# A fused hash-attention and squared-ReLU kernel on one core: an earlier place for the second pair's hash work, and another spread of the sums of the input weights

## The chip, the cores and the metric

The kernel runs on one core of a Trainium2 chip. The metric is the time of one execution on the device in microseconds (us); "the time" of a kernel is the median over several executions. A profile is one more execution, recorded by the hardware profiler; times inside it are counted from the start of its span. TensorE is the matrix engine (PE in the profile), VectorE is DVE, ScalarE is ACT, GpSimd is POOL, and SyncE (SP) issues most of the DMAs.

## What is computed

Attention in which a query sees only the keys that have the same hash bucket, and then a feed-forward block with a squared ReLU. Cut to what matters:

```python
q, k, v: (4, 8, 768, 64); proj: (64, 6); w_in: (512, 2048); w_out: (2048, 512)

q_bits = (q @ proj > 0);  k_bits = (k @ proj > 0)
mask   = bucket(q_bits)[:, None] == bucket(k_bits)[None, :]
scores = where(mask, (q @ k.T) / 8, -1e9)
attn   = softmax(scores)
x      = (attn @ v), reshaped to (3072, 512)
out    = square(maximum(x @ w_in, 0)) @ w_out
```

## The kernel before

**Stages.** The attention comes first: 32 heads (4 batches of 8), two at a time, so 16 pairs (`pr` 0 to 15), about 330 us of the 880. The feed-forward block follows, as fast matrix multiplications of Strassen's kind: blocks of the inputs are added and subtracted first, and seven products stand for eight. The sums of blocks of `w_in` that these products need are made during the attention: 16 of them, `sum_in(0)` to `sum_in(15)`, each one VectorE operation on 128x512 numbers (lines 516 and 533) and two DMAs that write it to memory (`put_factor`, line 203). A dictionary `sums`, built by the loop that the change touches, says in which pair each is made: from pair 4 on (`NIN // 2`), when the first half of the input weights is there; what is left is made in the last pair.

**Order.** All engines' work is written in program order by hand (`tc.manual_schedule()`), with one queue per engine; the loop over the pairs below is that order.

**One pair.** The keys are cut into six tiles of 128 (`kt` 0 to 5).
- `features(pr, w)` (line 333): VectorE transposes the queries (w=0) and keys (w=1) of a pair in 32x32 blocks, so that features lie along the partitions; `nat` holds what the DMAs loaded (`load_pair`, issued two pairs ahead; the loads of pair 1 are issued at the start).
- `hash_bits(pr, banks)` (line 346): eight TensorE products of features with `proj` into one PSUM buffer, tile name `hash`.
- `signs(pr, w)` (line 356): eight ScalarE operations that read that buffer and write `bits`, keys first. `weigh(pr)` (line 382) scales the keys' bits.
- `prepare()`: `hash_bits` and both `signs` of the next pair.
- `score(pr, kt)` (lines 396 and 413): TensorE products of bits and of features into PSUM, 512 queries and then 256, each followed by ScalarE's exponential into `e`, one of a ring of four. PSUM buffers for scores and hash products come from one set of three, called `turn`, used in rotation.
- `add_up(pr, kt)` (lines 423 and 428): VectorE adds the exponentials of the tiles into `total`.
- `attend(pr, kt)` (line 438): TensorE products of exponentials and values, into one PSUM buffer `xo`.
- `finish(pr - 1)`: in the next pair, `sum_up` adds `total` over the partitions (line 455, `tot`; VectorE's `flip`, `once` and `both`, lines 460 to 466), the last two tiles are attended, and `spread` (line 477) distributes the reciprocals; `normalize` (lines 487 and 493, `recs` and `x_t`) scales and stores the result. The next pair's first `attend` needs `xo` free again.
- Beside this, pieces of the weights, given as 64-bit floats, are turned into 32-bit ones: `part_weight` (VectorE, lines 143 and 147), `place_power` (ScalarE, `small` and `power`, lines 160 and 161) and `round_weight` (VectorE, lines 171 to 179), for two pieces in a pair, `a` and `b`.

In pair 0 the loop differs: the pair's own hash bits are made ahead of the loop and within it (`first_keys`), the features of pair 1 are transposed after `add_up(0, 1)`, and `prepare()` for pair 1 runs after `score(0, 3)`. In the later pairs `features(pr + 1)` stands at the top of the pair and `prepare` runs inside `finish`, after `score(pr, 1)`.

After the last pair come `sum_x(0, 1)`, `finish(15)`, `normalize(15)`, and then the feed-forward block (`product`, line 712, and others).

Of the kernel before, what the change touches and what calls it, by code (L numbers as in the profile page):

```python
# [34 lines left out]
def kernel(  # L35
# [22 lines left out]
    NP = B * H // 2  # L58
# [45 lines left out]
    def turn(name):  # L104

        return ps_s.tile([P, 2, 512], FP32, name=name, tag="turn")
# [4 lines left out]
    NIN = 2 * NFT  # L111
# [11 lines left out]
    def load_weight(i):  # L123
        src, r, c = pieces[i]
        if src.dtype != U64:
            goals[i] = goal(i)
            nc.sync.dma_start(out=goals[i], in_=src[r:r + P, c:c + PIECE])
            return
        raw = p_w.tile([P, PIECE, 2], U32, name="raw", bufs=3)
        nc.sync.dma_start(  # L130
            out=raw.rearrange("p f w -> p (f w)"),
            in_=src.bitcast(U32)[r:r + P, 2 * c:2 * (c + PIECE)],
        )
        raws[i] = raw
# [28 lines left out]
    def round_weight(i):  # L163

        raw = raws.pop(i, None)
        if raw is None:
            return keep_weight(i)
        goals[i] = goal(i)
        low, high = raw[:, :, 0], raw[:, :, 1]
        power, top = parts.pop(i)  # L170
        nc.vector.scalar_tensor_tensor(  # L171
            out=power, in0=high, scalar=0x80000000, in1=power,
            op0=ALU.bitwise_and, op1=ALU.bitwise_or,
        )
        one = top.bitcast(FP32)
        nc.vector.scalar_tensor_tensor(
            out=one, in0=low, scalar=2.0**-32, in1=top, op0=ALU.mult, op1=ALU.add,
        )
        nc.vector.scalar_tensor_tensor(  # L179
            out=goals[i], in0=one, scalar=2.0**-20, in1=power.bitcast(FP32),  # L180
            op0=ALU.mult, op1=ALU.mult,
        )
        keep_weight(i)
# [95 lines left out]
    def load_pair(pr):  # L279


        b, j = divmod(pr, PB)
        for src, name in ((q, "q_nat"), (k, "k_nat")):
            t = p_qk.tile([P, S], FP32, name=name)
            for g in range(4):
                h, e = divmod(g, 2)
                nc.sync.dma_start(
                    out=t[g * 32:(g + 1) * 32].rearrange("i (c d) -> i c d", d=32),
                    in_=src[b, 2 * j + h].rearrange("(c i) (e d) -> e i c d", i=32, e=2)[e],
                )  # L290
            nat[pr, name] = t
# [38 lines left out]
    def features(pr, w):  # L330

        feat[pr, w] = p_f.tile([P, S], FP32, name=f"feat{w}")
        nc.vector.transpose(out=feat[pr, w], in_=nat[pr, ("q_nat", "k_nat")[w]])
# [3 lines left out]
    def hash_bits(pr, banks, ws=(0, 1), cs=(0, 1)):  # L337


        for w in ws:  # L340
            hashed[pr, w] = banks
            for c in cs:
                g = 2 * w + c
                for h in range(2):
                    rows = slice(h * D, (h + 1) * D)
                    nc.tensor.matmul(  # L346
                        out=banks[g * NR_B:(g + 1) * NR_B, h, 0:HS], lhsT=projs[rows],
                        rhs=feat[pr, w][rows, c * HS:(c + 1) * HS], start=True, stop=True,
                    )

    def signs(pr, w):
        bits[pr, w] = t = all_bits[pr % 2][w]
        for c in range(2):
            at = slice((2 * w + c) * NR_B, (2 * w + c + 1) * NR_B)
            for h in range(2):
                nc.scalar.activation(  # L356
                    out=t[h * D:h * D + NR_B, c * HS:(c + 1) * HS], in_=hashed[pr, w][at, h, 0:HS],
                    func=ACTF.Sign, scale=HUGE, bias=lifts[at],
                )
# [19 lines left out]
    def weigh(pr):  # L379

        t = bits[pr, 1]
        nc.scalar.activation(out=t, in_=t, func=ACTF.Copy, scale=gains)
# [3 lines left out]
    def score(pr, kt):  # L386

        e = ring[len(weights) % NRING]
        weights[pr, kt] = e
        key = slice(kt * P, (kt + 1) * P)  # L390
        sts = []

        def products(st, lo, hi, src, first):
            for h in range(2):
                rows = slice(h * D, (h + 1) * D)
                nc.tensor.matmul(  # L396
                    out=st[:, h, 0:hi - lo], lhsT=src[pr, 1][rows, key],
                    rhs=src[pr, 0][rows, lo:hi], start=first, stop=not first,
                )


        if (pr, kt) == (0, 0):
            for lo, hi in CUTS:
                sts.append(turn("st"))
                products(sts[-1], lo, hi, feat, True)
        for i, (lo, hi) in enumerate(CUTS):
            if len(sts) <= i:
                sts.append(turn("st"))
                products(sts[i], lo, hi, bits, True)
                products(sts[i], lo, hi, feat, False)  # L410
            else:
                products(sts[i], lo, hi, bits, False)
            nc.scalar.activation(  # L413
                out=e[:, :, lo:hi], in_=sts[i][:, :, 0:hi - lo], func=ACTF.Exp, scale=scale
            )
# [106 lines left out]
    def sum_in(m):  # L522

        c, n = divmod(m, 4)
        j, h = divmod(c, 2)
        t, at = ins[j], slice(h * NS, (h + 1) * NS)
        nf = NFT // 2
        a11, a12, a21, a22 = (
            t[:, f:f + nf, g, at] for g in range(2) for f in (0, nf)
        )  # L530
        s = in_sums[m] = p_t.tile([P, nf, NS], FP32, name=f"s_in{n}", bufs=2)
        if n == 0:
            nc.vector.tensor_tensor(out=s, in0=a21, in1=a22, op=ALU.add)
        else:
            minus(s, *(
                (in_sums[4 * c], a11), (a11, a21), (a12, in_sums.get(4 * c + 1))
            )[n - 1])
        put_factor((3, 4, 5, 6)[n], c * NS, s)
# [4 lines left out]
    todo = list(range(16))  # L543
    sums = {}
    for pr in range(NIN // 2, NP):
        n = 16 if pr == NP - 1 else 1 + (pr == NIN + 1)
        sums[pr], todo = todo[:n], todo[n:]

    xs = {}
# [1 line left out]
    def load_x(i):  # L551

        x = p_c.tile([P, NFT, NCH], FP32, name="x")
        nc.gpsimd.dma_start(out=x, in_=x_all[:, :, i * NCH:(i + 1) * NCH])
        xs[i] = x, [p_c.tile([P, 2, NCH // 2], FP32, name=f"t_x{n}") for n in range(3)]
# [36 lines left out]
    with tc.manual_schedule():  # L592
# [21 lines left out]
        for pr in range(NP):  # L614
            a, b = 2 * pr, 2 * pr + 1
            more = pr + 1 < NP

            def prepare():

                hash_bits(pr + 1, turn("hash"))  # L620
                for w in (1, 0):
                    signs(pr + 1, w)


            if pr + 2 < NP:
                load_pair(pr + 2)
            if pr == X_0:
                load_x(0)
            if more and pr > 0:
                for w in range(2):  # L630
                    features(pr + 1, w)
            if pr > 0:
                round_weight(b - 2)
                load_weight(b)
                for m in sums.get(pr, ()):
                    sum_in(m)
            score(pr, 0)
            if pr == 0:
                first_keys(1, turn("hash"))
            score(pr, 1)  # L640
            if pr > 0:
                finish(pr - 1, prepare if more else None)
            add_up(pr, 1)
            if pr == 0:
                for w in range(2):
                    features(1, w)
            if pr > 0:
                normalize(pr - 1)


            if pr == X_0 + 1:
                for n in range(2):
                    load_unit(n)
            part_weight(a)
            score(pr, 2)
            score(pr, 3)
            if pr == 0:
                prepare()
            elif more:
                weigh(pr + 1)  # L660
            place_power(a)
            attend(pr, 0)
            attend(pr, 1)
            for kt in (2, 3):
                add_up(pr, kt)
            if more:
                load_values(pr + 1)


            round_weight(a)  # L670
            part_weight(b)
            if more:
                load_weight(a + 2)
            score(pr, 4)
            score(pr, 5)
            if pr == 0:
                weigh(1)
            place_power(b)
            attend(pr, 2)
            attend(pr, 3)  # L680
            add_up(pr, 4)
            add_up(pr, 5)
# [801 lines left out]
```

## Time and profile before

| | us |
|---|---|
| time, median of five executions | 882.1 |
| the five executions | 880.24, 881.27, 882.1, 882.57, 883.03 |
| the profiled execution, whole | 881.76 |
| its span | 880.0 |
| pair 0 and what comes before it (0 to 30.03) | 30.03, TensorE busy 25.99, VectorE 17.62, ScalarE 20.92 |
| a middle pair with one sum (169.30 to 189.20) | 19.90, TensorE 19.90, VectorE 19.16, ScalarE 17.07 |
| the pair with two sums (189.20 to 209.10) | 19.90, TensorE 19.90, VectorE 19.13, ScalarE 17.07 |
| the last pair (308.60 to 332.70) | 24.10, TensorE 23.06, VectorE 23.61, ScalarE 11.56 |

How to read it: a row gives a stretch of the span and how long each engine was busy in it. An engine that is busy for the whole stretch sets its length; where none is, something waits for something else, and the timeline says for what. Lines of the timeline give the start, the duration, the engine, the line of the program, the operation, what it writes and reads, how many instructions of this kind stand together, and in brackets how long the engine was idle before it and what ended the idle time. Lines of a list of waits give who waited for whom, the sum in us, how often, and the longest. Matmul ends are modelled, and neighbours overlap.

### The profile page before, as it was taken

The numbers are of one execution on the slowest core, as the hardware profiler recorded it, in microseconds if no ns is written. First come the engines' busy times: TensorE is split into PE (matmuls) and PEld (weight loads), VectorE is DVE, ScalarE is ACT, GpSimd is POOL, SyncE is SP. The second block draws the span as 40 slices with busy tenths as digits, with TensorE's granted clock in tenths as the row PEclk, the third lists the DMA queues.
The fourth block names the chain that finished last, engine by engine and source line by source line (L and its number), as shares of the span: only waits on it lengthen the run. The fifth ranks groups of instructions, "written<-read, shape, count | busy, mean of one in ns | idle before, by whom it ended". The sixth has DMA issues, their size and how long they took to land.

```text
span 880.0 us, 12132 instructions
## 1 busy us (share of the span) xinstructions
PE 865.2 (98%) x4340; PEld 519.4 (59%) x4340; DVE 760.8 (86%) x1099; ACT 391.6 (45%) x673; POOL 106.9 (12%) x172
## 2 busy tenths in 40 slices
PE   8999999999999999999999999999999999999996
PEld 3444444444444444444688865556888755568885
DVE  5899999999999998888779968888889788888875
ACT  5988888888888851222211123332111233321110
POOL 2000000000000000554231011111000211210002
PEclk9999999999999999999999999999999999999999
DMA  9678976898778536989897665436857744355565
GB/s 184 128 150 135 231 151 150 180 260 219 180 168 221 164 124 205 302 260 289 290 350 246 177 158 173 166 117 226 287 146 189 169 162 156 125 167 154 157 176 103
DMA packets 224131, 167.09 MB, mean 190 GB/s; under 512 B 164448, under 2 KB 181344, under 8 KB 224064
## 3 DMA queue, kind: packets, MB, share of 16 engines
q1 hardware_dynamic: 189152, 87.19, 40.9%
q0 software_dynamic: 12528, 41.30, 15.2%
q10 hardware_dynamic: 22384, 37.76, 13.8%
q8 instruction: 36, 0.59, 0.3%
q14 instruction: 31, 0.25, 0.1%
HBM read 124.52 MB, written 41.68 MB: 189 GB/s over the span
## 4 chain that ended last, share of the span: by engine, by line
PE 94%; DVE 2%; ACT 1%; issue 1%; DMA 1%; ACTq 0%; DVEq 0%
PE acc L712 40%; PE st L396 17%; PE acc L931 16%; PE xo L438 13%; PE acc L884 5%; PE hash L346 1%; PE tot L455 1%; DVE total L428 1%; DMA k_nat<-in_k_dram 1%; ACT e L413 1%; ACT bits L356 1%; DVE s_in L516 0%; DVE out_piece L179 0%; DVE power L171 0%; ACT small L160 0%
## 5 line engine op out<-in xcount | busy, mean ns | idle before, releaser
L413 ACT ACTIVATE e<-st 128x1024 f32<-128x1024 f32 x192 | 145.1, 810 | 45.0 <-PE st L396 41.0
L396 PE MATMUL st<-feat,feat 64*128 64x512 f32 (+1 forms) x768 | 150.4, 483 | 0.0
L438 PE MATMUL xo<-e,v_nat 128*64 128x512 f32 (+1 forms) x768 | 134.8, 492 | 0.0
L712 PE MATMUL acc<-b,leaf 128*128 128x256 f32 x600 | 133.2, 379 | 1.3 <-issue 1.3
L712 PEld LDWEIGHTS acc<-b,leaf 128*128 128x128 f32 x600 | 113.8, 190 | 17.7 <-issue 2.3
L428 DVE TENSOR_TENSOR total<-total,e 128x1536 f32<-128x1536 f32 x64 | 112.4, 1756 | 5.2 <-ACT small L160 0.5
L438 PEld LDWEIGHTS xo<-e,v_nat 128*64 128x64 f32 x768 | 51.3, 136 | 82.4 <-issue 74.6
L931 PE MATMUL acc<-t_x,w_unit 128*128 128x512 f32 x192 | 90.2, 592 | 0.0
L396 PEld LDWEIGHTS st<-feat,feat 64*128 64x128 f32 x768 | 66.0, 188 | 33.3 <-issue 23.4
L712 PE MATMUL acc<-t,leaf 128*128 128x256 f32 x336 | 76.2, 380 | 0.0
L356 ACT ACTIVATE bits<-hash,lifts 32x384 bf16<-32x384 f32 x120 | 68.6, 572 | 3.2 <-issue 1.3
L712 PEld LDWEIGHTS acc<-t,leaf 128*128 128x128 f32 x336 | 63.7, 190 | 9.1 <-DVE t L516 0.5
L796 DVE SCALAR_TENSOR_TENSOR b<-h 128x512 f32<-128x512 f32 x96 | 65.7, 691 | 3.0
L396 PE MATMUL st<-bits,bits 64*128 64x256 bf16 (+1 forms) x384 | 63.2, 325 | 1.8 <-ACT e L413 1.4
L931 PE MATMUL acc<-x,w_unit 128*128 128x512 f32 x128 | 60.1, 592 | 0.0
L712 PE MATMUL acc<-x,w_unit 128*128 128x512 f32 x128 | 56.6, 594 | 0.0
L712 PE MATMUL acc<-b_t,leaf 128*128 128x256 f32 x240 | 53.8, 379 | 0.0
L931 PEld LDWEIGHTS acc<-t_x,w_unit 128*128 128x128 f32 x192 | 36.5, 190 | 28.9 <-issue 26.8
L719 ACT COPY two<-acc 128x256 f32<-128x256 f32 (+1 forms) x29 | 12.5, 431 | 87.8 <-PE acc L712 75.3
L719 ACT COPY one<-acc 128x256 f32<-128x256 f32 (+1 forms) x29 | 12.5, 431 | 86.3 <-PE acc L712 48.3
L712 PEld LDWEIGHTS acc<-b_t,leaf 128*128 128x128 f32 x240 | 45.5, 190 | 6.2
L396 PEld LDWEIGHTS <-bits 64*128 64x128 bf16 x384 | 23.5, 93 | 42.0 <-issue 37.9
(159 smaller groups left out, 1166.9 us busy)
## 6 DMA issues: line engine op xcount, KB each, us to landing
leaf<-w_out ACTq DMA_DIRECT2D x142, 256.0 KB, 3.0
w_unit<-w_in SPq DMA_DIRECT2D x16, 640.0 KB, 3.9
raw<-in_moe_w_in_dram SPq DMA_DIRECT2D x16, 512.0 KB, 5.5
raw<-in_moe_w_out_dram SPq DMA_DIRECT2D x16, 512.0 KB, 4.4
w_unit<-w_in SPq DMA_DIRECT2D x8, 896.0 KB, 8.0
w_out<-sums POOLq DMA_DIRECT2D x16, 448.0 KB, 6.8
sum<-w_in SPq DMA_DIRECT2D x16, 448.0 KB, 4.8
v_nat<-in_v_dram SPq DMA_DIRECT2D x16, 384.0 KB, 4.8
```

The source lines that it names most:

```text
L346: nc.tensor.matmul(out=banks[g * NR_B:(g + 1) * NR_B, h, 0:HS], lhsT=projs[rows], rhs=feat[pr, w][rows, c * HS:(c + 1) * HS], start=True, ...
L356: nc.scalar.activation(out=t[h * D:h * D + NR_B, c * HS:(c + 1) * HS], in_=hashed[pr, w][at, h, 0:HS], func=ACTF.Sign, scale=HUGE, bias=li ...
L396: nc.tensor.matmul(out=st[:, h, 0:hi - lo], lhsT=src[pr, 1][rows, key], rhs=src[pr, 0][rows, lo:hi], start=first, stop=not first,)
L413: nc.scalar.activation(out=e[:, :, lo:hi], in_=sts[i][:, :, 0:hi - lo], func=ACTF.Exp, scale=scale)
L428: nc.vector.tensor_tensor(out=totals[pr], in0=totals[pr], in1=weights[pr, kt][:, :, 0:S], op=ALU.add)
L438: nc.tensor.matmul(out=xo[h * D:(h + 1) * D, lo:hi], lhsT=nat[pr, "v_nat"][:, h, kt * D:(kt + 1) * D], rhs=weights[pr, kt][:, h, lo:hi], s ...
L455: nc.tensor.matmul(out=tot[g * 32:(g + 1) * 32, 0:HS], lhsT=ones, rhs=totals[pr][:, h, c * HS:(c + 1) * HS], start=True, stop=True,)
L712: nc.tensor.matmul(out=acc[to], lhsT=a(i), rhs=b(i), start=first and i == 0, stop=last and i == n - 1, skip_group_check=True,)
L719: nc.scalar.copy(out=t, in_=acc[of])
L796: nc.vector.scalar_tensor_tensor(out=out, in0=h, scalar=0.0, in1=h, op0=ALU.max, op1=ALU.mult)
L884: nc.tensor.matmul(out=out, lhsT=w[:, a], rhs=b, start=start, stop=stop, skip_group_check=True)
L931: nc.tensor.matmul(out=acc[to], lhsT=w[:, PLACE[a], f], rhs=bt[b](f), start=first and f == 0, stop=last and f == NFT // 2 - 1, skip_group_ ...
```

## The change

Three edits in the order of the work. First, the loop that builds `sums`: before, the pair `NIN + 1` (index 9, the tenth) makes two sums and every other one from index 4 to 14 makes one, which leaves four for the last. After, the pairs with an index divisible by three (6, 9 and 12) make two, which leaves two for the last. Second, in pair 0 the two `features` of pair 1 move ahead of `add_up(0, 1)` on VectorE. Third, in pair 0 `prepare()` for pair 1 moves ahead of `score(0, 3)`: on TensorE the eight hash products come before the products of tile 3, on ScalarE the eight signs before its two exponentials. The instructions are the same in number and kind on every engine.

```diff
     for pr in range(NIN // 2, NP):
-        n = 16 if pr == NP - 1 else 1 + (pr == NIN + 1)
+        n = 16 if pr == NP - 1 else 1 + (pr % 3 == 0)
         sums[pr], todo = todo[:n], todo[n:]
...
             score(pr, 1)
+            if pr == 0:
+                for w in range(2):
+                    features(1, w)
             if pr > 0:
                 finish(pr - 1, prepare if more else None)
             add_up(pr, 1)
-            if pr == 0:
-                for w in range(2):
-                    features(1, w)
             if pr > 0:
                 normalize(pr - 1)
...
             part_weight(a)
             score(pr, 2)
-            score(pr, 3)
             if pr == 0:
                 prepare()
-            elif more:
+            score(pr, 3)
+            if more and pr > 0:
                 weigh(pr + 1)
             place_power(a)
             attend(pr, 0)
```

## The prediction

> **What bounds the kernel now.** I read the engine totals and the chain that ended last, then all that TensorE waited for in the whole run, then the timelines of single engines around those waits.
>
> ```profile
> PE 865.2 (98%) x4340; PEld 519.4 (59%) x4340; DVE 760.8 (86%) x1099; ACT 391.6 (45%) x673; POOL 106.9 (12%) x172
> ...
> PE 94%; DVE 2%; ACT 1%; issue 1%; DMA 1%; ACTq 0%; DVEq 0%
> ```
>
> TensorE is the kernel. A change of order pays only where TensorE stands still; here is the complete list:
>
> ```profile
> PE xo L326 <- DVE excess L235: 1.5, 1, 1.5
> PE st L396 <- ACT e L413: 1.4, 2, 1.2
> PE acc L712 <- issue: 1.3, 1, 1.3
> PE tot L455 <- DVE total L428: 1.0, 1, 1.0
> PE acc L1039 <- DVE o L1008: 0.8, 1, 0.8
> PE hash L346 <- ACT e L413: 0.6, 1, 0.6
> PE st L396 <- ACT bits L356: 0.4, 1, 0.4
> ```
>
> Lines 2, 6 and 7 (2.4 us) are in the first pair, line 4 (1.04 us) is the end of the last pair. Between them TensorE has no gap at all: the sums of a pair (L455) begin every 19.91 us, thirteen times on end (34.31 to 293.10). So the first half of the change can gain a part of 2.4 us, the second half a part of 1.04 us, and nothing else is to be had. First pair, ScalarE, then VectorE:
>
> ```profile
> 13.32 4.75 ACT L413 ACTIVATE e<-st 128x1024 f32<-128x1024 f32 x6 [0.85 <-PE st L396]
> 19.39 4.66 ACT L356 ACTIVATE bits<-hash,lifts 32x384 bf16<-32x384 f32 x8 [1.33 <-issue]
> 24.08 0.72 ACT L160 ACTIVATE small<-power,excess 128x512 uint8<-128x512 uint32 x1
> ```
>
> ```profile
> 13.01 0.38 DVE L374 TENSOR_SCALAR bits<-bits,spans,bases 128x384 bf16<-128x384 bf16 x1
> 14.86 1.76 DVE L423 SCALAR_TENSOR_TENSOR total<-e,e 128x1536 f32<-128x1536 f32 x1 [1.48 <-ACT e L413]
> ...
> 17.43 0.94 DVE L333 STREAM_TRANSPOSE feat<-k_nat 128x768 f32<-128x768 f32 x1
> ...
> 25.50 0.69 DVE L171 SCALAR_TENSOR_TENSOR power<-raw,power 128x512 uint32<-128x512 uint32 x1 [2.95 <-ACT power L161]
> ...
> 32.53 0.94 DVE L333 STREAM_TRANSPOSE feat<-k_nat 128x768 f32<-128x768 f32 x1
> ```
>
> The reader is to see: VectorE waits 1.48 us for an exponential and only then transposes the next pair's features; so the hash products come late, ScalarE idles 1.33 us before their signs, and everything queued behind the signs (small, power, the exponential of tile 4 at 25.49) is late; TensorE waits 1.21 us for that exponential. Last pair, VectorE and TensorE:
>
> ```profile
> 312.80 0.69 DVE L516 TENSOR_TENSOR s_in<-in 128x512 f32<-128x512 f32 x1
> 313.40 0.68 DVE L516 TENSOR_TENSOR s_in<-in,s_in 128x512 f32<-128x512 f32 x1
> 314.00 0.58 DVE L460 STREAM_TRANSPOSE flip<-tot 128x384 f32<-128x384 f32 x1
> ...
> 316.64 0.98 DVE L487 STREAM_TRANSPOSE recs<-xo 128x768 f32<-128x768 f32 x1
> ...
> 319.26 3.62 DVE L428 TENSOR_TENSOR total<-total,e 128x1536 f32<-128x1536 f32 x2
> ```
>
> ```profile
> 329.07 0.85 PE L455 MATMUL tot<-total,ones 128*32 128x384 f32 x8 [1.04 <-DVE total L428]
> ```
>
> From 309.54 to 329.02 VectorE runs with no pause above 0.1 us: here it sets the end.
>
> **What the Trainium skill says.** "PSUM — Partial Sum Buffer", section Engine vs sequencer instructions: ScalarE's and VectorE's queues are strict FIFO, and matmuls start and complete in program order. The trace agrees: small (24.08) and the tile-4 exponential stand behind the eight signs although tile 4's products were done at 23.7. "VectorE: DVE Perf Modes", section The TRN2 errata: an fp32 tensor_tensor takes (N+151)/0.96 ns; that is 691 for N=512 and 1757 for 1536, and the rows have 0.69 and 1.76. "ScalarE: Activation LUTs", section What ACT_TABLE_LOAD costs: neighbouring ACTIVATEs overlap by about 93 ns. The exponentials do (0.11: 13.32+1.03 against 14.24), the signs do not (eight of 0.572 take 4.66).
>
> **First pair, step by step.** Nothing is added or removed: two transposes, eight hash products and eight signs move. VectorE: the two transposes go ahead of L423. It is free at 13.39; the two take 1.83 (16.54 to 18.37), so they end at 15.25. Their inputs: the last k_nat DMA was issued at 8.3 and the tile's DMAs took 3.6 to 5.6, so it is there by 13.9 at worst. TensorE: the products of tile 2 are issued by 15.26, when the hash products now come; they take 0.81 (292.29 to 293.10 in pair 14). Their PSUM turn (three buffers) is the one that tile 1's second exponential left at 14.83. They are done at about 16.2, and tile 3's products follow at 16.1, when tile 2's first exponential has freed a turn (15.96). ScalarE: tile 2's exponentials end at 16.45, signs from 16.48 to 21.14 (4.66), tile 3's exponentials to 22.69, small from 22.57 (they overlap by 0.1), power from 23.33, tile 4's first exponential from 23.98 to 25.01. Before it ended at 26.52. TensorE meanwhile: tile 3 to 17.8, attention products of tiles 0 and 1 (2.74) to 20.5; then a new wait, as tile 4's turn is the hash turn: to 21.19, 0.6 us, hidden because the wait behind it is longer. The second half of tile 5 starts at 25.06 against 26.57: **1.51 us sooner**.
>
> But the exponentials of tile 3 are now behind the signs, and VectorE's add of tile 3 (second L428) waits for them: 22.72 to 24.48, in place of 20.79 to 22.55. L171 behind it starts at 24.39, not 25.50: VectorE gains only **1.11**. From there to the transposes of pair 2 it runs without a break (25.50 to 33.47), so these end at 32.36. TensorE reaches the hash products of pair 2 at 33.30-1.51 = 31.79; its key half started at 33.53 before (0.23 behind the query half, at 33.30) and will start at 32.42, 0.63 behind. So 0.40 of the gain is given back and TensorE follows VectorE: 1.11 us. Bounds: 1.51 if key features don't hold TensorE there, 0.7 if the signs start 0.4 later than I think (several semaphores in one wait). I take 1.11.
>
> **Pairs 7, 10, 13.** The tenth has two sums before and after. A sum costs VectorE 0.60 start to start (313.40 to 314.00), ahead of the flip. What hides it: VectorE has some 0.75 us to spare in a 19.91 us pair (19.15 busy), and the trace has the very case: in the tenth pair with two sums, both ended at 196.01 and its reader on TensorE (L477) began at 196.98; x_t ended at 199.63, the attention products that need its bank began at 200.51; the next L455 came after 19.91 as ever. Margins 0.97 and 0.88. So nothing for the seventh and thirteenth, at most 0.3 each if they lie worse. On SP two more small issues (0.90 for two at 134.74) stand ahead of the x_all write and the v_nat load; the values are read a pair later. POOL's order is the same.
>
> **Last pair.** Two of four sums go, 1.2 us of VectorE. The flip can't come before the sums' products: L455 at 312.20, and in pairs 2 to 8 the flip starts 0.91 to 0.92 after it, so at 313.12: 0.88 gained. recs needs L477, which TensorE does at 315.62, 0.30 before recs in pair 14 (296.51, 296.81): 315.92, 0.72 gained. x_t, L143, L147 follow to 318.54; the add of tile 2 needs the exponential that ends at 318.61 (ScalarE, paced by TensorE): 318.65 against 319.26, **0.61 gained**. Afterwards nothing bites: power is ready at 321.50 (needed 322.19), tile 4's exponential at 324.69 (needed 324.79), tile 5's at 326.31 (needed 326.65). The sums' products start at 328.46; TensorE is free at 328.03, so 0.43 of its wait stays. Bounds: 0.3 to 1.04, the whole wait.
>
> **Sum.** 1.11 + 0 + 0.61 = 1.72 off the span of 880.0: 878.28. The profiled execution took 881.76, 1.76 outside the span, so 880.04; it lay 0.34 below the median of 882.1, from which 1.72 leaves 880.4. That is 0.195%, all but at the 0.2% (1.76 us) that a measurement of this kernel can tell from no change. The later stages keep their order on every engine and shift as a whole.
>
> **Rivals.** *More:* the key half of pair 2's hash isn't on the path, because later matmuls absorb its 0.4 us. For it: TensorE lists no wait there before. Against: L455 of that pair came 0.78 after the key half, as tight as can be. 1.51+0.61 = 2.12: 880.0. With the whole last wait gone too, 879.5. *Only one half bites:* the last pair's adds are held by ScalarE alone, or the first pair's gain is eaten by VectorE's lag: 0.6 to 1.1, 881.0 to 881.5. For: both gains are what is left after a second wait. *Slower:* the hash products now stand ahead of tile 3 on TensorE and the signs ahead of tile 3's exponentials on ScalarE. If k_nat or VectorE is late, both queues stop, one for one once the key products end after 16.4. At 18.1 the total gain is gone; with the old feature times they end at 19.3 to 20.1, some 3.7 late: 2 us slower, 884.1. Against: the data are there 1.2 to 1.3 us early by the median landing (3.9).
>
> **How the numbers follow.** Forecast 0.58, more 0.25, one half 0.10, slower 0.07. A spread of half a microsecond around 880.4 puts the forecast's weight evenly on both sides of the bound: 0.28 faster, 0.30 same. More is faster (0.24; 0.01 same); one half is same (0.10). Faster 0.52, same 0.41, slower 0.07. The bounds of the unknown costs give gains of 1.0 to 2.55, so 879.5 to 881.1; the five runs before lay from 880.24 to 883.03, which moves a median by some 0.7 either way: 878.8 to 881.9.
>
> **What would show it.** Right: TensorE's waits in the first pair some 0.6 and 1.0 at tile 4 and the second half of tile 5, none at the hash; signs starting at about 16.5; pair 2's L455 at about 33.2; later L455s 19.91 apart; the last wait about 0.4. Wrong: signs after 17.5, a gap before tile 3, a wait at pair 7 or 13, or an L455 of pair 2 at 32.8 (then "more").

## The result, and the profile after

The changed kernel takes 879.68 us (median of 22 executions) against 881.49 us for the kernel before (43 executions). The ratio is 0.9979, with a 95% interval from 0.9974 to 0.9985: 1.8 us less, 0.21%. The forecast was 1.72 us less.

First the list of all that TensorE waited for in the changed kernel (who waited for whom, sum in us, times, longest):

```profile
PE xo L326 <- DVE excess L235: 1.5, 1, 1.5
PE st L396 <- ACT e L413: 1.2, 2, 1.0
PE acc L1039 <- DVE o L1008: 0.8, 1, 0.8
PE tp L309 <- DMA k_nat<-in_k_dram: 0.8, 1, 0.8
PE acc L712 <- issue: 0.6, 1, 0.6
PE st L396 <- ACT bits L356: 0.5, 1, 0.5
PE tot L455 <- DVE total L428: 0.4, 1, 0.4
```

The wait ahead of the hash products is gone. The one for the signs (0.4 before, 0.5 now) has moved from tile 5 to tile 4. Both start as soon as the signs are done with reading a PSUM buffer: at 24.11 before (signs until 24.05), at 21.24 now (signs until 21.19). At the end of the last pair 0.4 of 1.04 us is left. A new line, 0.8 us for the keys at the very start, and a smaller one in the feed-forward block (L712: 0.6 instead of 1.3) differ between executions of one kernel, as the last experiment and the last section show.

The timeline of ScalarE in the first pair:

```profile
13.37 3.13 ACT L413 ACTIVATE e<-st 128x1024 f32<-128x1024 f32 x4 [0.85 <-PE st L396]
16.52 4.67 ACT L356 ACTIVATE bits<-hash,lifts 32x384 bf16<-32x384 f32 x8
21.21 1.51 ACT L413 ACTIVATE e<-st 128x1024 f32<-128x1024 f32 x2
22.75 0.72 ACT L160 ACTIVATE small<-power,excess 128x512 uint8<-128x512 uint32 x1
```

ScalarE no longer idles ahead of the signs; they start at 16.52 instead of 19.39. But tile 3's two exponentials (21.21; before, they were done at 18.07) now stand behind them. VectorE shows who waits for those:

```profile
13.37 0.97 DVE L333 STREAM_TRANSPOSE feat<-q_nat 128x768 f32<-128x768 f32 x1
14.27 0.94 DVE L333 STREAM_TRANSPOSE feat<-k_nat 128x768 f32<-128x768 f32 x1
...
22.76 1.76 DVE L428 TENSOR_TENSOR total<-total,e 128x1536 f32<-128x1536 f32 x1 [3.58 <-ACT e L413]
24.43 0.69 DVE L171 SCALAR_TENSOR_TENSOR power<-raw,power 128x512 uint32<-128x512 uint32 x1
...
31.48 0.94 DVE L333 STREAM_TRANSPOSE feat<-k_nat 128x768 f32<-128x768 f32 x1
```

VectorE waits 3.58 us for tile 3, adds it, and L171 follows at once, without a wait of its own: the add holds it. The key transposes of pair 2 end at 32.42. TensorE before:

```profile
17.66 1.62 PE L346 MATMUL hash<-feat,projs 64*32 64x384 f32 x16 [0.60 <-ACT e L413]
...
24.11 0.39 PE L396 MATMUL st<-bits,bits 64*128 64x512 bf16 x2 [0.37 <-ACT bits L356]
...
26.57 0.29 PE L396 MATMUL st<-bits,bits 64*128 64x256 bf16 x2 [1.21 <-ACT e L413]
...
33.30 1.08 PE L346 MATMUL hash<-feat,projs 64*32 64x384 f32 x16
34.31 0.85 PE L455 MATMUL tot<-total,ones 128*32 128x384 f32 x8
```

And after:

```profile
15.42 0.88 PE L346 MATMUL hash<-feat,projs 64*32 64x384 f32 x16
...
21.24 0.39 PE L396 MATMUL st<-bits,bits 64*128 64x512 bf16 x2 [0.48 <-ACT bits L356]
...
25.10 0.29 PE L396 MATMUL st<-bits,bits 64*128 64x256 bf16 x2 [0.99 <-ACT e L413]
...
31.83 1.49 PE L346 MATMUL hash<-feat,projs 64*32 64x384 f32 x16
33.25 0.85 PE L455 MATMUL tot<-total,ones 128*32 128x384 f32 x8
```

Tile 5's second half starts 1.47 us sooner (25.10 against 26.57). The listed waits between `first_keys` and there have shrunk by only 0.73 us (from 2.42 to 1.69). The other 0.74 was inside the hash products of pair 1, which took 1.62 us before and take 0.88 now: their key half waited for VectorE's transposes (it started at 18.43, the transposes ended at 18.37), and the list of waits does not show a stop within such a group.

The hash products of pair 2, though, stretch over 1.49 us instead of 1.08, as their key half (from 32.47) waits for the transposes, and L455 is 1.06 sooner (33.25 against 34.31). From there every pair takes what it took: thirteen steps of 19.91. In the last pair, VectorE and then TensorE:

```profile
311.01 0.68 DVE L516 TENSOR_TENSOR s_in<-in,s_in 128x512 f32<-128x512 f32 x1
312.06 0.58 DVE L460 STREAM_TRANSPOSE flip<-tot 128x384 f32<-128x384 f32 x1 [0.37 <-PE tot L455]
...
314.85 0.98 DVE L487 STREAM_TRANSPOSE recs<-xo 128x768 f32<-128x768 f32 x1
...
317.59 3.62 DVE L428 TENSOR_TENSOR total<-total,e 128x1536 f32<-128x1536 f32 x2
```

```profile
327.40 0.85 PE L455 MATMUL tot<-total,ones 128*32 128x384 f32 x8 [0.43 <-DVE total L428]
```

The flip now waits for TensorE: VectorE has more time than it can use here. The last L455 comes at 327.40 (329.07 before), so 0.61 is added to the 1.06. The spans differ by more, 2.3 us (880.0 and 877.7): beside these 1.67 us, the L712 gap is 0.72 smaller.

### The profile page after: what moved, and what is told of

Same layout as the page of the kernel before. It is cut to its first block, busy times and chain, and to the rows that moved or that the text cites. A ratio compares the mean times of both kernels' runs of the same rounds, so it can differ in the third digit from the quotient of the medians.

```text
span 877.7 us, 12130 instructions
## 1 busy us (share of the span) xinstructions
PE 864.4 (98%) x4340; PEld 518.6 (59%) x4340; DVE 760.4 (87%) x1099; ACT 391.5 (45%) x673; POOL 107.0 (12%) x172
## 4 chain that ended last, share of the span: by engine, by line
PE 95%; DVE 2%; ACT 1%; DMA 1%; issue 0%; ACTq 0%; DVEq 0%
PE acc L712 40%; PE st L396 17%; PE acc L931 16%; PE xo L438 14%; PE acc L884 6%; PE hash L346 2%; PE tot L455 1%; DVE total L428 1%; DMA k_nat<-in_k_dram 1%; ACT bits L356 1%; ACT e L413 0%; PE xo L477 0%; DVE x_t L493 0%; PE tp L309 0%; DVE recs L487 0%
## 5 line engine op out<-in xcount | busy, mean ns | idle before, releaser
L712 PE MATMUL acc<-b,leaf 128*128 128x256 f32 x600 | 133.3, 379 | 0.6 <-issue 0.6
L712 PEld LDWEIGHTS acc<-b,leaf 128*128 128x128 f32 x600 | 113.8, 190 | 17.2 <-issue 1.9
L712 PE MATMUL acc<-t,leaf 128*128 128x256 f32 x336 | 76.2, 380 | 0.0
L712 PEld LDWEIGHTS acc<-t,leaf 128*128 128x128 f32 x336 | 63.7, 190 | 9.1 <-DVE t L516 0.5
L712 PE MATMUL acc<-x,w_unit 128*128 128x512 f32 x128 | 56.6, 594 | 0.0
L712 PE MATMUL acc<-b_t,leaf 128*128 128x256 f32 x240 | 53.8, 379 | 0.0
L712 PEld LDWEIGHTS acc<-b_t,leaf 128*128 128x128 f32 x240 | 45.5, 190 | 6.2
```

Of the source, the lines that this page charges most:

```text
L712: nc.tensor.matmul(out=acc[to], lhsT=a(i), rhs=b(i), start=first and i == 0, stop=last and i == n - 1, skip_group_check=True,)
```

## Experiments

Pair 0 gets going up to 0.6 us sooner in one execution than in another (the last section shows how), and all of it shifts with that. The table therefore counts from the start of the second hash product group of pair 0 (`first_keys`, at 10.96 before). All numbers are from the timelines, in us; the last two columns are the first step between two L455, and TensorE's wait ahead of the last L455.

| kernel | `first_keys` at | tile 5, second half | L171 | first L455 | first step | last wait |
|---|---|---|---|---|---|---|
| before | 10.96 | 15.61 | 14.54 | 23.35 | 19.91 | 1.04 |
| the change | 11.02 | 14.08 | 13.41 | 22.23 | 19.91 | 0.43 |
| sums only | 10.95 | 15.60 | 14.53 | 23.33 | 19.91 | 0.42 |
| first pair only | 11.46 | 14.09 | 13.42 | 22.22 | 19.91 | 1.03 |
| features only | 11.45 | 14.29 | 13.23 | 22.03 | 19.91 | 0.42 |
| next features sooner | 11.22 | 14.07 | 13.41 | 21.61 | 20.27 | 0.43 |

Six profiles are of kernels with the first pair as in the change: it itself, first pair only, and the last four below. Their first L455 lies at 22.20 to 22.25, so a difference of less than 0.05 says nothing.

### The two halves apart

Sums only: the kernel before with

```diff
-        n = 16 if pr == NP - 1 else 1 + (pr == NIN + 1)
+        n = 16 if pr == NP - 1 else 1 + (pr % 3 == 0)
```

> The kernel before with the other spread of the sums alone. Theory (two separate gains that add up): pair 0 as before, sums of pair 1 (L455) first at about 34.3 us, fourteen intervals unchanged, TensorE's wait ahead of the last L455 down from 1.04 to 0.43 us, so 0.6 us less in all, ratio about 0.9993. Rival (one half carries all): ratio 1.000, the wait at the last L455 still 1.0, because VectorE starts the last pair late when TensorE is not ahead.

Measured: ratio 0.9995 (0.9987 to 1.0004); the last wait falls from 1.04 to 0.42, everything before it stays. First pair only: the changed kernel with that line turned back.

> The changed kernel with the sums as in the kernel before. Theory: TensorE's waits in pair 0 are 0.5 and 1.0, none at the hash products; first L455 at about 33.25 (before: 34.31), all later ones 1.06 us sooner than before, last wait 1.04 as before; 1.06 us less, ratio about 0.9988. Rival (VectorE's lag from pair 0 grows when the last pair keeps four sums): last wait above 1.04 and less than 1 us gained.

Measured: ratio 0.9986 (0.9978 to 0.9995); first L455 1.13 sooner in the table, last wait 1.03. The halves add up, 0.62 and 1.13, and neither needs the other. The time alone could not have said so for the sums: its interval holds no change, and only the wait shows the gain.

### The third edit alone taken back

```diff
             score(pr, 2)
+            score(pr, 3)
             if pr == 0:
                 prepare()
-            score(pr, 3)
```

> The changed kernel with the hash products and signs of pair 1 back behind tile 3, so of the first-pair edits only the earlier transposes are left; sums as in the change. Theory (VectorE's add of tile 3 behind the signs gives back 0.4 us): signs start at about 18.1 us instead of 19.39, tile 5's second half at about 25.3, VectorE's L171 at about 24.2, and the first L455 at about 33.0, that is some 0.2 us sooner than in the full change (33.25): the third edit loses on balance. Rival (the third edit carries the gain, TensorE's time in pair 0 decides): tile 5's second half 0.2 us later than in the full change and the first L455 at 33.45 or later.

Measured: ratio 0.9978 (0.9971 to 0.9985). VectorE in the first pair of this kernel:

```profile
17.86 3.62 DVE L428 TENSOR_TENSOR total<-total,e 128x1536 f32<-128x1536 f32 x2
24.68 0.69 DVE L171 SCALAR_TENSOR_TENSOR power<-raw,power 128x512 uint32<-128x512 uint32 x1 [3.20 <-ACT power L161]
```

The two adds run together again, and L171 waits for ScalarE's power. In the table tile 5 is 0.21 later than with the full change, as the rival has it, and L171 0.18 and L455 0.20 sooner, as the theory has it. (Times from the span's start are some 0.45 above the expected ones, since pair 0 began 0.49 later. L455 at 33.48 would meet the rival's "33.45 or later" for this reason alone.) So the earlier transposes bring 1.32 us by themselves. The third edit helps TensorE by 0.21 in pair 0 and costs VectorE 0.18, and VectorE is what counts one pair later: by these profiles the change would be 0.2 us better without it. The times do not tell the two kernels apart (879.57 and 879.68); the statement rests on the profiles.

### The features of the pair after that, sooner too

```diff
-            if more and pr > 0:
+            if more and pr > 1:
                 for w in range(2):
                     features(pr + 1, w)
...
+            if pr == 0:
+                for w in range(2):
+                    features(2, w)
             add_up(pr, 4)
             add_up(pr, 5)
```

> The changed kernel with the transposes of pair 2's features moved from the top of pair 1 to before the adds of tiles 4 and 5 in pair 0. Theory (in pair 1 TensorE follows VectorE's transposes, which ate 0.4 us): hash products of pair 2 no longer split in two halves, first L455 at about 32.65 instead of 33.25, later ones the same 0.6 us sooner, ratio to the kernel before about 0.9972. Rival (the key half of the hash was not on the path, or the adds of tiles 4 and 5 now come too late for L455): first L455 stays at 33.2 or goes later, ratio 0.998 or above.

Measured: ratio 0.9978 (0.9971 to 0.9985). TensorE in pair 1 of this kernel:

```profile
32.02 0.88 PE L346 MATMUL hash<-feat,projs 64*32 64x384 f32 x16
32.83 0.85 PE L455 MATMUL tot<-total,ones 128*32 128x384 f32 x8
...
36.66 1.02 PE L396 MATMUL st<-feat,feat 64*128 64x512 f32 x4
37.87 0.29 PE L396 MATMUL st<-bits,bits 64*128 64x256 bf16 x2 [0.19 <-ACT bits L356]
```

The hash products take 0.88 in one piece, and L455 is another 0.62 sooner: the key half was on the path, as forecast. But the next step is 20.27, so 0.36 is given back. Tile 2's second half (37.87) now waits for the signs of pair 2, which end at 37.82; it starts 1.21 us after the products before it. In the changed kernel:

```profile
37.08 1.02 PE L396 MATMUL st<-feat,feat 64*128 64x512 f32 x4
37.94 0.27 PE L396 MATMUL st<-bits,bits 64*128 64x256 bf16 x2
```

There the same products start after 0.86 us, although the signs run until 38.07. In the trace that instruction waits for a semaphore that ScalarE raises here, and for one that TensorE raises in the change. So it has probably been given another of the three PSUM buffers, the one that the signs still read. Net gain over the change by the profile 0.26; in the time it does not show (879.73).

### How many sums the pairs can hide

None in the last pair, two in each pair of odd index from 5 to 13:

```diff
-        n = 16 if pr == NP - 1 else 1 + (pr % 3 == 0)
+        n = 16 if pr == NP - 1 else 1 + pr % 2
```

> The changed kernel with two sums in every pair of odd index from 5 to 13 (the sixth to the fourteenth pair), none in the last. Theory (in the last pair two sums are already hidden: the flip waits for TensorE's L455, then recs for L477, then the adds for the exponentials): flip of the last pair but one still 0.92 after its L455, last wait still 0.43, no gain over the change. Rival (each sum taken from the last pair is worth its 0.6 us): the last wait gone, another 0.4 us and more. In the pairs with two sums L455 steps of 19.91 as ever.

Measured: ratio 0.9982 (0.9975 to 0.9989), all steps 19.91, last wait 0.43. VectorE in the last pair:

```profile
310.10 0.69 DVE L179 SCALAR_TENSOR_TENSOR out_piece<-top,power 128x512 f32<-128x512 f32 x1
312.36 0.58 DVE L460 STREAM_TRANSPOSE flip<-tot 128x384 f32<-128x384 f32 x1 [1.57 <-PE tot L455]
```

The flip's wait grew from 0.37 to 1.57 by just the two sums (1.20), and nothing else moved: those two were hidden, as the forecast had it. Three in the last pair (two in the seventh and tenth alone):

```diff
-        n = 16 if pr == NP - 1 else 1 + (pr % 3 == 0)
+        n = 16 if pr == NP - 1 else 1 + (pr in (6, NIN + 1))
```

> The changed kernel with two sums in the seventh and tenth pair only, so three in the last. Theory (three sums end at 313.4 on the clock of the kernel before, 0.3 after the flip could start, and later waits swallow that): last wait 0.43 to 0.5, so nearly all of the gain with one sum moved instead of two. Rival (0.3 us for each sum): last wait 0.7.

Measured: ratio 0.9982 (0.9974 to 0.999), last wait 0.43. One sum moved out of the last pair had all of the gain; the second brought nothing. Four in the tenth pair, one in the others, two in the last:

```diff
-        n = 16 if pr == NP - 1 else 1 + (pr % 3 == 0)
+        n = 16 if pr == NP - 1 else 1 + 3 * (pr == NIN + 1)
```

> The changed kernel with four sums in the tenth pair and one in each other pair from the fifth to the fourteenth, two in the last. Theory (0.6 us a sum, margins of 0.97 and 0.88 with two): with two more sums VectorE comes 1.2 us later, past both margins, so the spread products (L477) and the first attention products of that pair wait, and the one L455 step behind the tenth pair is 20.2 to 20.3 instead of 19.91; all others 19.91. Rival (VectorE has hidden room for any number, as it waits for exponentials anyway): 19.91 there too.

Measured: ratio 0.9987 (0.9978 to 0.9996); the step behind the tenth pair is 20.28, all others 19.91. VectorE there, then TensorE:

```profile
194.41 0.68 DVE L533 TENSOR_TENSOR s_in<-in 128x512 f32<-128x512 f32 x1
195.01 0.57 DVE L460 STREAM_TRANSPOSE flip<-tot 128x384 f32<-128x384 f32 x1
...
198.66 1.02 DVE L493 SCALAR_TENSOR_TENSOR x_t<-xo,recs 128x768 f32<-128x768 f32 x1
```

```profile
196.12 0.30 PE L477 MATMUL xo<-both,picks 128*64 128x24 f32 x4
...
199.74 2.81 PE L438 MATMUL xo<-e,v_nat 128*64 128x512 f32 x16
```

Four sums are past the cover: L477 starts at 196.12 behind `both` (195.88 to 196.06), and the attention products at 199.74, after x_t's end at 199.68. Two sums beyond the two are 1.20 us of VectorE and cost 0.37, so 0.83 was covered, near the smaller of the two margins forecast (0.88), and the rival with room for any number falls. Three sums in such a pair were not run.

### The changed kernel once more

> The changed kernel unchanged, for a second profile of it. Theory (the gap ahead of a product of the feed-forward block near 450 us and the first arrival of the keys at 6.5 us differ from run to run and have nothing to do with the change): L455 steps and waits in the pairs as in the first profile within 0.02 us, that gap somewhere from 0.5 to 1.3, the second first_keys product from 10.9 to 11.5. Rival (the change moved the gap): again 0.58 within 0.05.

Measured, in one execution: steps and waits in the pairs as in the first profile (first L455 22.23 after `first_keys`; waits of 0.49, 0.99 and 0.42). TensorE's wait for the keys, 0.8 in the first profile, is not in the list. The L712 gap was 0.97, against 0.58 in the first profile.

```profile
PE acc L712 <- issue: 1.0, 1, 1.0
```

So 0.4 of the 2.3 us between the two spans lies within what that gap does between two executions of the same kernel. That the rest of its 0.72 is chance too is likely, not shown: the changed kernel had 0.58 and 0.97, the kernel before 1.30 in its one profile, but sums only 0.90, and four in the tenth 1.63. What TensorE waits for there the profile does not show ("issue").

## Why the prediction was right

- *The first pair's VectorE and ScalarE.* Predicted: key features done at 15.25, signs from 16.48, tile 4's exponential from 23.98. Measured 15.21, 16.52 and 24.04. The closeness of the last is part luck: small and power came 0.18 later than forecast (22.75 and 23.51), since small did not overlap the exponentials before it, and the exponential then began 0.10 before power's end, which was not forecast. The two waits left on TensorE were put at 0.6 and 1.0; they are 0.48 and 0.99, with the first one, new at tile 4, hidden behind the second as forecast.
- *The list called complete.* The prediction took 2.4 us as all that the first half could gain. That is wrong both ways: 0.24 of it lies at tile 1 (12.03 before, 0.22 left after), which no edit touches, and 0.74 within the hash products of pair 1 is not in the list. The forecast did not suffer, as it was worked out along ScalarE's queue.
- *The part of the gain that is given back.* Predicted: TensorE gains 1.51, VectorE 1.11, and TensorE follows VectorE at the hash products of pair 2. Measured on the table's clock 1.53, 1.13 and 1.12. Features only and next features sooner show the cause from both sides: freeing L171 from tile 3's add moves L455 by 0.20 although TensorE is later, and taking the transposes off the path moves it by 0.62. The rival "more" falls with that: later matmuls do not absorb the key half's delay.
- *Double sums in the seventh and thirteenth pair.* Priced at nothing; all steps stayed at 19.91. Four sums in one pair show that the cover was real and limited.
- *The last pair.* Predicted 0.61 of a possible 1.04: the flip would then wait for TensorE, recs for L477, and the add of tile 2, last, for ScalarE's exponential. On the clock of the kernel before (1.06 added) they were put at 313.12, 315.92 and 318.65, and came at 313.12, 315.91 and 318.65. The gain is 0.61; the kernels with none and three in the last pair confirm that it is the later waits that set the number.
- *The sum.* 1.72 forecast, 1.81 between the medians. In the profile the parts named make 1.67 (1.06 and 0.61), on the table's clock 1.73 (1.12 and 0.61); the interval of the ratio, 1.3 to 2.3 us, holds them all. The time itself was forecast at 880.4 and is 879.68: the forecast was counted from a median of five executions, 882.1, and that of 43 is 881.49. The result lies just beyond the 0.2% that the prediction took for the least that can be told from no change, with that bound inside its interval. But that interval reaches only 0.05 to 0.06% to either side, so with 22 and 43 executions less than 0.2% can be told from no change.
- *The slower rival.* It needed late key data or a late VectorE; the hash products started at 15.42 behind tile 2 with no gap, and no run here had them late, so what late keys would cost was not tested.

That the other buffer is what made the step of 20.27 is inferred from the semaphores waited for and two timelines; no kernel tested it.

## What to carry to other kernels

Price an order change by the engine that the next shared wait hangs on, not by the engine whose wait disappears: here TensorE came to the end of pair 0 1.5 us sooner, but 1.1 us came out, because the same change put an exponential late for VectorE, and TensorE met VectorE again a pair later. Read how long a group of products takes beside the list of waits: 0.74 us of TensorE's standing still was in no line of it. Before work is moved off the engine that sets a stage's end, find the next input of each step behind it; one of the two moved operations was worth 0.6 us and the other nothing. Where an effect is below what the times resolve, steps between like instructions in the profile, counted from a common event, still tell kernels apart to 0.05 us.

## What the runs showed of the hardware

Two stretches differ between executions whatever the kernel. The second `first_keys` group started between 10.87 and 11.46 us in the ten profiles here. Two things moved it. The first keys landed between 6.4 and 7.0 us. And the six TensorE products that transpose the first queries (line 309) took 0.42 us each in four profiles, 0.27 in two, and some of each in four. The second execution of the changed kernel and none in the last both had the keys at 6.4, but their groups started at 10.87 and 11.34: in the first most of these products were at 0.27, in the second all at 0.42. The gap ahead of an L712 product near 450 us had sizes from 0.58 to 1.63 us. A span of one profile is therefore worth no more than about a microsecond in a comparison, while the steps of 19.91 us between them repeat to 0.01.
